# Strassen's seven block products in the first layer of the second expert pair, on one Trainium2 core

## The chip, the cores and the metric

The kernel runs on one core of one Trainium2 chip, as one program. The metric is the device time of one execution in microseconds (us); lower is better. Runs of the kernel before took 1161.63, 1161.28 and 1159.16 us, median 1161.28 us.

## What is computed

Retention over 768 steps for 4 x 8 heads of width 64, followed by two feed-forward layers ("expert pairs") on the 3072 resulting tokens of width 512:

```
state = gamma * state + k_t v_t^T ;  y_t = scale * q_t state        (per head)
x = y as 3072 tokens x 512
h = x @ w_in  (512 -> 2048);  g = h - tanh(h);  x = g @ w_out       (first pair)
h = x @ w2_in (512 -> 2048);  g = elu(h);       out = g @ w2_out    (second pair)
```

Inputs and outputs are float32. The four weight matrices arrive as doubles' bit patterns (int64), and the kernel makes float32 of them.

## The kernel before

Every float32 product is made of three float32r products: each operand is split into a high part (ACT copies it to float32r) and a low part (DVE subtracts the copy), and TensorE adds high x high, high x low and low x high in PSUM. Three matmuls of 128x128 by 128x512 therefore stand for one.

The 3072 tokens are six groups of 512 (`NB`), the 2048 hidden columns 16 pieces of 128 (`NF`). One *slot* is one group and one piece: `first_mm` (L268 to L279) makes h with 12 matmuls (four chunks of the inner size 512, three each), ACT and DVE make g of it (`act_tanhshrink` L289, `act_elu` L310), `split_hi` and `split_lo` (L281 to L287) split g, and `second_mm` (L328 to L343) adds g times the piece's row of the outer weights into four PSUM accumulators with 12 more matmuls. `second_mm` of a slot runs two slots behind `first_mm` (`SKEW`). There are 96 slots in each pair. In the first pair the slots of groups 0 and 1 are cut in two halves of eight pieces (`FA`), so that weights can be converted while they arrive.

The main loop (L577 to L619) writes the instructions of each engine in the order of the slots, and every engine runs its own list in that order, waiting on semaphores. Retention steps 4 to 23 are spread over the slots of the first pair by a table (`events`, L526 to L542): step s makes scores on TensorE (L164), masks on DVE (L172), outputs (L208, L215) and a state update (L237, L260, L263) for which the keys are scaled first (`att_scale_k`, L145). Steps 0 to 3 and the conversion of the first weights stand ahead of the loop, written out by hand (L399 to L502).

Weights are fetched (L81), converted on ACT and DVE (L86, L93, L94), split (L106, L107) and then stay in on-chip memory: one tag per piece for the inner and one for the outer weights, so that the second pair's weights replace the first pair's piece by piece during the last token group of the first pair. Between the pairs the tokens go through DRAM (`x1d`), and are loaded and split again, one group ahead (`load_x1` L380, `split_x1` L386). PSUM has eight banks: four accumulators, two for h, two for retention. All loads and stores are issued from SP's queue, except two that add into DRAM (POOL) and four tables (ACT).

The line at which the last output leaves is L359 behind the copies of L353.

Of the kernel before, what the change touches and what calls it, by code (L numbers as in the profile page):

```python
# [7 lines left out]
F32 = mybir.dt.float32  # L8
# [29 lines left out]
def retention_moe_kernel(ctx: ExitStack, tc: tile.TileContext, dims, ins, out):  # L41
# [10 lines left out]
    assert H * D == DM and 2 * D == P and B == SPB and NB == NCH and S % P == 0  # L52

    const = ctx.enter_context(tc.tile_pool(name="const", bufs=1))
    wp = ctx.enter_context(tc.tile_pool(name="wp", bufs=1))
    xp = ctx.enter_context(tc.tile_pool(name="xp", bufs=1))
    stg = ctx.enter_context(tc.tile_pool(name="stg", bufs=4))
    att = ctx.enter_context(tc.tile_pool(name="att", bufs=2))
    att1 = ctx.enter_context(tc.tile_pool(name="att1", bufs=1))
    tmp = ctx.enter_context(tc.tile_pool(name="tmp", bufs=1))  # L60
    ps_acc = ctx.enter_context(tc.tile_pool(name="ps_acc", bufs=1, space=PSUM))
    ps_h = ctx.enter_context(tc.tile_pool(name="ps_h", bufs=2, space=PSUM))
    ps_a = ctx.enter_context(tc.tile_pool(name="ps_a", bufs=1, space=PSUM))
# [8 lines left out]


    wts = {}
    raw = {}
    w32 = {}

    def fetch(m, f):

        raw[m, f] = wp.tile([P, TB], I64, tag=f"w{m % 2}_{f}", name=f"raw{m}_{f}")  # L80
        nc.sync.dma_start(out=raw[m, f], in_=ins[f"w{m}"][f])  # L81

    def convert_a(job):

        w = w32[job] = stg.tile([P, TB], F32, tag="w32", name=f"w32_{job[0]}_{job[1]}")
        nc.scalar.activation(out=w, in_=raw[job].bitcast(F32)[:, 1::2], func=AF.Prelu, scale=REBIAS, alpha=NEG)  # L86

    def convert_b(job):

        r, w = raw[job].bitcast(U32), w32[job]  # L90
        wu = w.bitcast(U32)
        return [
            lambda: nc.vector.tensor_single_scalar(wu, wu, 3, op=ALU.logical_shift_left),  # L93
            lambda: nc.vector.scalar_tensor_tensor(  # L94
                out=wu, in0=r[:, 0::2], scalar=29, in1=wu,
                op0=ALU.logical_shift_right, op1=ALU.bitwise_or,
            ),
        ]
# [12 lines left out]

    xhl = {}
    st = {}
    qkv_t = {}
    pt_t = {}

    def bank(s, part):

        tag = {"sc0": "a0", "sc1": "a1", "o": "a0"}[part]
        if s < B:  # L120
            tag = [("a0", "a1", "acc0"), ("acc1", "acc2", "acc3")][s % 2][("sc0", "sc1", "o").index(part)]
        return ps_acc if tag[:3] == "acc" else ps_a, tag

    def att_load(s, qk):
        nc.sync.dma_start(out=qk, in_=ins["qkv"][s][:, 0:2, :])
        qkv_t[s] = [qk, None, None]

    def att_load_v(s):
        v = att.tile([P, TB], F32, tag="v", bufs=B, name=f"v{s}")
        nc.sync.dma_start(out=v, in_=ins["qkv"][s][:, 2, :])  # L130
        qkv_t[s][1] = v

    def att_scale_q(s):
        q = qkv_t[s][0][:, 0, :].rearrange("p (a i) -> p a i", a=NP)
        nc.vector.tensor_tensor(out=q, in0=q, in1=qtab, op=ALU.mult)

    def att_load_kn(s, kn=None):
        if s // B == NCH - 1:
            return
        if kn is None:  # L140
            kn = att.tile([P, TB], F32, tag="kn", name=f"kn{s}")
        nc.sync.dma_start(out=kn, in_=ins["qkv"][s][:, 3, :])
        qkv_t[s][2] = kn

    def att_scale_k(s):  # L145
        if s // B == NCH - 1:
            return
        k = qkv_t[s][2].rearrange("p (h d) -> p h d", h=H)
        nc.vector.tensor_tensor(out=k, in0=k, in1=ktab.to_broadcast([P, H, D]), op=ALU.mult)

    def att_scores(s):
        t = qkv_t[s][0]
        if s < B:
            pt = tmp.tile([P, 2, NP, P], F32, tag="g", bufs=G_BUFS, name=f"pt{s}")
        else:
            pt = att1.tile([P, 2, NP, P], F32, tag="pt", name=f"pt{s}")
        sc = []
        for j in range(2):
            pool, tag = bank(s, f"sc{j}")
            sc.append(pool.tile([P, NP, P], F32, tag=tag, name=f"sc{s}_{j}"))  # L160
        for p in range(NP):
            for j in range(2):
                r = slice(j * D, (j + 1) * D)
                nc.tensor.matmul(  # L164
                    out=sc[j][:, p, :],
                    lhsT=t[r, 1, p * P:(p + 1) * P],
                    rhs=t[r, 0, p * P:(p + 1) * P],
                    start=True, stop=True,
                )
# [517 lines left out]
```

## Time and profile before

| | |
|---|---|
| median of three runs | 1161.28 us |
| the runs | 1161.63, 1161.28, 1159.16 us |
| span of the profiled execution | 1159.1 us (the page gives no other time of it; the nearest run is 1159.16) |
| TensorE (PE) busy | 1138.6 us, 98% |
| VectorE (DVE), ScalarE (ACT) busy | 684.6 us (59%), 625.2 us (54%) |
| moved by DMA | 80.44 MB, mean 69 GB/s |

The span runs from the first to the last instruction. A busy share is a mean over stages that differ; what a stage waits for is read in that stage, from the windows, the timeline and the waits. Matmuls overlap: the mean duration of one (about 390 ns) is longer than the distance between the starts of two, and only that distance adds up to time.

### The profile page before, as it was taken

The page shows a single profiled execution, that of the slowest core. Times are in us where ns is not written, and L with a number is a line of the kernel's source. Part 1 is how long each engine was busy: PE and PEld are TensorE (multiplying, and loading weights), DVE is VectorE, ACT ScalarE, POOL GpSimd, SP SyncE. Part 2 cuts the span into 40 slices and gives each one's busy share as a digit, 9 for nine tenths or more (in the row PEclk, how much of TensorE's full clock was granted, in tenths as well). Part 3 has the DMA queues.
Part 4 walks back from the last instruction along what each step waited for, and adds up shares of the span by engine and source line. Part 5 has one row for each costly group of instructions (what it writes and reads, how often), then busy time and mean ns, then how long its engine had stood idle before and what let it go on. Part 6 is the DMA issues. An engine that isn't in the chain of part 4 may idle for free.

```text
span 1159.1 us, 15702 instructions
## 1 busy us (share of the span) xinstructions
PE 1138.6 (98%) x6033; PEld 929.9 (80%) x6033; DVE 684.6 (59%) x1153; ACT 625.2 (54%) x1117; POOL 5.6 (0%) x10
## 2 busy tenths in 40 slices
PE   7799999999999999999999999999999999999998
PEld 5578887888888888888888888888888888888886
DVE  6898887657666665665798675343343343343332
ACT  2657785445545455455787765444444444444434
POOL 0000001000000000000000000000000000000000
PEclk9899999999999999999999999999999999999999
DMA  9930032431103102001675200200200200200000
GB/s 329 416 155 37 1 110 51 132 72 38 38 1 109 38 28 92 28 1 32 206 234 166 90 1 1 72 1 1 72 1 1 72 1 1 73 1 1 36 1 37
DMA packets 27562, 80.44 MB, mean 69 GB/s; under 512 B 3168, under 2 KB 3168, under 8 KB 27488
## 3 DMA queue, kind: packets, MB, share of 16 engines
q1 hardware_dynamic: 26048, 76.56, 19.0%
q0 software_dynamic: 864, 2.10, 1.2%
q8 instruction: 47, 0.77, 0.3%
q10 hardware_dynamic: 576, 0.79, 0.2%
q14 instruction: 27, 0.22, 0.1%
HBM read 64.76 MB, written 14.68 MB: 69 GB/s over the span
## 4 chain that ended last, share of the span: by engine, by line
PE 93%; DMA 3%; DVE 2%; ACT 0%; issue 0%; SPq 0%; DVEq 0%; ACTq 0%
PE acc L340 45%; PE h L274 43%; DMA raw<-w 2%; PE sc L164 2%; PE oe L215 1%; PE oe L208 1%; PE oo L215 1%; DMA stage<-qkv 1%; PE oo L237 1%; DMA dtab<-dtab 1%; DVE w L94 0%; DVE w L107 0%; SPq L81 0%; DVE v L307 0%; DVE x L227 0%
## 5 line engine op out<-in xcount | busy, mean ns | idle before, releaser
L340 PE MATMUL acc<-g,w 128*128 128x512 f32 x1152 | 282.0, 393 | 0.0
L274 PE MATMUL h<-x,w 128*128 128x512 f32 x1152 | 278.3, 391 | 0.0
L340 PE MATMUL acc<-w,g 128*128 128x512 f32 x1152 | 276.7, 389 | 0.6 <-DVE g L287 0.6
L274 PE MATMUL h<-y,w 128*128 128x512 f32 x1152 | 276.7, 389 | 0.0
L274 PEld LDWEIGHTS h<-x,w 128*128 128x128 f32 x1152 | 216.8, 188 | 45.5 <-issue 0.2
L340 PEld LDWEIGHTS acc<-w,g 128*128 128x128 f32 x1152 | 216.1, 188 | 45.9 <-DVE g L287 1.0
L274 PEld LDWEIGHTS h<-y,w 128*128 128x128 f32 x1152 | 216.2, 188 | 44.9
L340 PEld LDWEIGHTS acc<-g,w 128*128 128x128 f32 x1152 | 213.3, 188 | 47.3 <-ACT v L295 0.7
L320 DVE SCALAR_TENSOR_TENSOR v<-v,t 128x512 f32<-128x512 f32 x96 | 66.5, 693 | 298.7 <-ACT t L318 298.7
L315 ACT ACTIVATE u<-h 128x512 f32<-128x512 f32 x96 | 57.5, 599 | 259.5 <-PE h L274 258.1
L294 ACT ACTIVATE u<-h 128x512 f32<-128x512 f32 x96 | 57.5, 599 | 235.5 <-issue 224.4
L300 DVE SCALAR_TENSOR_TENSOR v<-v,u 128x512 f32<-128x512 f32 x96 | 66.5, 692 | 135.1 <-ACT v L295 135.1
L287 DVE TENSOR_TENSOR g<-v,g 128x512 fp32r<-128x512 f32 x192 | 131.5, 685 | 0.8 <-ACT g L283 0.8
L283 ACT ACTIVATE g<-v 128x512 fp32r<-128x512 f32 x192 | 118.2, 615 | 3.3 <-DVE v L323 2.0
L307 DVE COPY_PREDICATED v<-m,h 128x512 f32<-128x512 uint16 x96 | 70.4, 734 | 4.8 <-DVE h L306 0.5
L295 ACT ACTIVATE v<-u,qa_b 128x512 f32<-128x512 f32 x96 | 69.5, 724 | 3.1
L303 DVE SCALAR_TENSOR_TENSOR v<-v,h 128x512 f32<-128x512 f32 x96 | 65.6, 683 | 9.4 <-ACT t L297 9.4
L298 ACT ACTIVATE m<-u,xs_b 128x512 bf16<-128x512 f32 x96 | 68.3, 712 | 0.0
L306 DVE TENSOR_TENSOR h<-h,t 128x512 f32<-128x512 f32 x96 | 66.5, 693 | 0.0
L323 DVE TENSOR_TENSOR v<-h,v 128x512 f32<-128x512 f32 x96 | 65.7, 684 | 0.0
L316 ACT ACTIVATE v<-u 128x512 f32<-128x512 f32 x96 | 60.7, 632 | 3.1
L318 ACT ACTIVATE t<-u 128x512 f32<-128x512 f32 x96 | 59.3, 618 | 0.0
(54 smaller groups left out, 617.9 us busy)
## 6 DMA issues: line engine op xcount, KB each, us to landing
raw<-w SPq DMA_DIRECT2D x64, 512.0 KB, 5.6
qk<-qkv SPq DMA_DIRECT2D x20, 512.0 KB, 5.3
v<-qkv SPq DMA_DIRECT2D x24, 256.0 KB, 6.3
x<-x1d SPq DMA_DIRECT2D x12, 512.0 KB, 5.9
kn<-qkv SPq DMA_DIRECT2D x20, 256.0 KB, 6.0
out<-o SPq DMA_DIRECT2D x10, 512.0 KB, 2.9
x1d<-o SPq DMA_DIRECT2D x8, 512.0 KB, 3.0
stage<-qkv SPq DMA_DIRECT2D x4, 512.0 KB, 6.8
```

Of the source, the lines that this page charges most:

```text
L274: nc.tensor.matmul(out=h, lhsT=w[:, a, c * P:(c + 1) * P], rhs=x[:, b, c, :], start=(i == 0), stop=(i == 3 * KC - 1),)
L283: nc.scalar.activation(out=t[:, 0, :], in_=g, func=AF.Copy)
L287: nc.vector.tensor_tensor(out=t[:, 1, :], in0=g, in1=t[:, 0, :].bitcast(F32), op=ALU.subtract)
L295: nc.scalar.activation(out=v, in_=u, func=AF.Square, bias=qa_b)
L298: nc.scalar.activation(out=big, in_=u, func=AF.Relu, bias=xs_b)
L300: lambda: nc.vector.scalar_tensor_tensor(out=v, in0=v, scalar=QB, in1=u, op0=ALU.add, op1=ALU.mult),
L303: lambda: nc.vector.scalar_tensor_tensor(out=v, in0=v, scalar=C2, in1=h, op0=ALU.mult, op1=ALU.mult),
L306: lambda: nc.vector.tensor_tensor(out=h, in0=h, in1=th, op=ALU.subtract),
L307: lambda: nc.vector.copy_predicated(out=v, mask=big.bitcast(U16), data=h),
L320: lambda: nc.vector.scalar_tensor_tensor(out=v, in0=v, scalar=1.0, in1=th, op0=ALU.add, op1=ALU.mult),
L323: lambda: nc.vector.tensor_tensor(out=v, in0=h, in1=v, op=ALU.max),
L340: nc.tensor.matmul(out=acc[e], lhsT=lhsT, rhs=rhs, start=(f == lo and i == 0), stop=(f == hi - 1 and i == 2),)
```

## The change

The first layer of the second pair is computed for pairs of token groups and pairs of pieces at once. The tokens of groups 2p and 2p+1 are regrouped: the first halves of both groups make one block row of 512 tokens, the second halves the other; the inner size 512 is cut in two halves of 256, and pieces j and j+8 are the two block columns. The 2x2 block product is done with Strassen's seven products (in Winograd's form, with 15 additions) in place of eight. Each of the seven has two inner chunks of 128, so six matmuls. There are 3 pairs x 8 *quads* x 7 products.

- The sums of the weights (T1 to T4) and all splits are made once, in the third to sixth token group of the first pair (`weight_quad`), and written to DRAM (`w2d`); each quad loads its 14 blocks (1.8 MB) into one of two buffers in each of the three pairs.
- The sums of the tokens (S1 to S4) are made when a pair's tokens are loaded (`tokens`): seven operands, each split in a high and a low part.
- The sums of the products are made partly in PSUM (P1, P6, P5 and P3 add up in one bank) and partly by three copies to SBUF on ACT (`snap`) and three additions on DVE (`plus`) per quad.
- A quad gives four h blocks. The two of the first block row go at once through elu, split and the second layer (12 matmuls each, called tails, one quad later). The two of the second block row are stored after elu (`ys`) and go through split and second layer after the eighth quad, in 16 units of 12 matmuls.
- The outer weights of both pairs (`w1d`, `w3d`) are converted and split once, stored to DRAM, and loaded again for each use: 64 loads for groups 2 to 5 of the first pair, 96 for the second pair, five buffers each.
- The order of everything behind the hand-written start is no longer that of the code: the code records operations with their operands, durations and due times (`Plan.op`), TensorE's in a fixed order, and `Plan.run` lays out the other engines' operations by their latest useful start, as engines, buffers and operands come free in its own clock. What the hand-written start has fetched counts there as present at its time zero. TensorE's order in the first pair is the one of before.

The core of the new code (L643 and on; `op` records, `dma` records a transfer):

```diff
+        def weight_store(job, d):
+            t = W[job]
+            dma(lambda: nc.sync.dma_start(out=d.bitcast(F32), in_=t.ap.bitcast(F32)), 4096, r=[t], w=[dbuf(d)], due=FAR)
...
+            op("DVE", q, lambda: sub(T(0), hi_.ap[:, 0:HW], lo_.ap[:, 0:HW]), r=[lo_, hi_], w=[(t, 0)], name="T1")
+            op("DVE", q, lambda: sub(T(1), hi_.ap[:, HW:], T(0)), r=[hi_, (t, 0)], w=[(t, 1)], name="T2")
+            op("DVE", q, lambda: sub(T(2), hi_.ap[:, HW:], hi_.ap[:, 0:HW]), r=[hi_], w=[(t, 2)], name="T3")
+            op("DVE", q, lambda: sub(T(3), lo_.ap[:, HW:], T(1)), r=[lo_, (t, 1)], w=[(t, 3)], name="T4")
...
+            op("DVE", 1.14, lambda: sub(s3.ap, a11.ap, a21.ap), r=[a11, a21], w=[s3], name="S3")
+            op("DVE", 1.14, lambda: add(a21.ap, a21.ap, a22.ap), r=[a22], w=[a21], name="S1")
+            op("DVE", 1.14, lambda: sub(a21.ap, a21.ap, a11.ap), r=[a11], w=[a21], name="S2")
+            op("DVE", 1.14, lambda: sub(a21.ap, a12.ap, a21.ap), r=[a12], w=[a21], name="S4")
...
+        def product(i, q, xs, dst, first, last):
+            h, l = xs[i]
+            k = PLACE[i]
+            def fn():
+                for c in range(2):
+                    three(dst.ap, lambda a: q.ap[:, 7 * a + k, c * P:(c + 1) * P],
+                          lambda b: (h, l)[b].ap[:, c, :], first, last, 2, c)
...
+                xb, wb, zb = (Buf("P", [P, TB], F32, f"{c}{nm}") for c in "xwz")
+                product(1, q, xs, xb, True, True)
+                s1 = snap(xb, f"s1_{nm}")
+                product(2, q, xs, wb, True, True)
+                c11 = plus(wb, s1, f"c11_{nm}")
+                product(6, q, xs, xb, False, True)
+                u2 = snap(xb, f"u2_{nm}")
+                product(7, q, xs, zb, True, True)
+                z7 = snap(zb, f"z7_{nm}")
+                product(5, q, xs, xb, False, True)
+                c22 = plus(xb, z7, f"c22_{nm}")
+                product(4, q, xs, zb, False, True)
+                c21 = plus(zb, u2, f"c21_{nm}")
+                y11 = elu(c11, f"11{nm}")
+                g = split_g(y11, f"11{nm}")
+                if j < NQ - 1:
+                    filler()
+                product(3, q, xs, xb, False, True)
+                y12 = elu(xb, f"12{nm}")
+                g2 = split_g(y12, f"12{nm}")
+                elu(c21, f"21{nm}", ys, 0, 0)
+                elu(c22, f"22{nm}", ys, 1, 1)
+                filler()
```

**Place one: TensorE, one quad (the sixth of the middle pair).** Names: x1_5, w1_5 and z1_5 are the quad's three PSUM banks, xh and xl the high and low part of a token operand (xh6 is S2), q1_5 the weight blocks, acc3a the accumulators of the tails. Before, the same stretch of the second pair alternates 12 matmuls of h and 12 into the accumulators:

```order
L274 MATMUL h2_120_6697<-y1_5997,w2_8_5435 128x512 x12
L340 MATMUL acc112_0_6496<-w3_6_5977,g118_6679 128x512 x3
L340 MATMUL acc112_1_6497<-w3_6_5977,g118_6679 128x512 x3
L340 MATMUL acc112_2_6498<-w3_6_5977,g118_6679 128x512 x3
L340 MATMUL acc112_3_6499<-w3_6_5977,g118_6679 128x512 x3
```

Now, the third and fourth product of the quad and the beginning of the first tail:

```order
L392 MATMUL x1_5_8023<-xh6_1_7288,q1_5_7881 128x512
L392 MATMUL x1_5_8023<-xl6_1_7302,q1_5_7881 128x512
L392 MATMUL x1_5_8023<-xh6_1_7288,q1_5_7881 128x512 x2
L392 MATMUL x1_5_8023<-xl6_1_7302,q1_5_7881 128x512
L392 MATMUL x1_5_8023<-xh6_1_7288,q1_5_7881 128x512
L392 MATMUL z1_5_8063<-xh7_1_7205,q1_5_7881 128x512
L392 MATMUL z1_5_8063<-xl7_1_7211,q1_5_7881 128x512
...
L392 MATMUL acc3a1_0_7605<-w3_4_7922,g111_4_7975 128x512 x3
L392 MATMUL acc3a1_1_7610<-w3_4_7922,g111_4_7975 128x512 x3
```

A product is six matmuls in place of the twelve of an h, and a tail uses the g of the quad before.

**Place two: ACT, the same quad.** s1, u2 and z7 are the copies out of PSUM, u, y, t the three steps of an elu, g a split's high part; 111, 121, 211 and 221 are the four blocks of the middle pair. Before, each slot has four ACT instructions:

```order
L315 ACTIVATE u143_7570<-h2_143_7557 128x512
L316 ACTIVATE v143_7572<-u143_7570 128x512
L283 ACTIVATE g142_7575<-v142_7536 128x512
L318 ACTIVATE t143_7571<-u143_7570 128x512
L315 ACTIVATE u144_7606<-h2_144_7593 128x512
```

Now, from the first copy of the quad to the copy of z7:

```order
L288 ACTIVATE s1_1_5_8046<-x1_5_8023 128x512
L744 ACTIVATE ys1_4_8030<-u221_4_8020 128x512
L744 ACTIVATE t221_4_8057<-u221_4_8020 128x512
L744 ACTIVATE u111_5_8061<-s1_1_5_8046 128x512
L288 ACTIVATE u2_1_5_8070<-x1_5_8023 128x512
L744 ACTIVATE y111_5_8073<-u111_5_8061 128x512
L744 ACTIVATE t111_5_8083<-u111_5_8061 128x512
L288 ACTIVATE z7_1_5_8085<-z1_5_8063 128x512
```

The three copies stand between the steps of elus, and u2 stands behind the first step of c11 (which DVE makes in the tile of s1).

**Place three: DVE at the end of the hand-written start.** kn5 are the keys of retention step 5, v0 or y0 the first slot's value, w32 a weight before its split. Before:

```order
L94 SCALAR_TENSOR_TENSOR w32_1_0_349<-raw1_0_149,w32_1_0_349 128x512
L300 SCALAR_TENSOR_TENSOR v0_403<-v0_403,u0_401 128x512
L93 TENSOR_SCALAR w32_0_3_407<-w32_0_3_407 128x512
L303 SCALAR_TENSOR_TENSOR v0_403<-v0_403,h0_0_361 128x512
L93 TENSOR_SCALAR w32_1_1_409<-w32_1_1_409 128x512
```

Now:

```order
L316 SCALAR_TENSOR_TENSOR w32_1_0_368<-raw1_0_168,w32_1_0_368 128x512
L343 TENSOR_TENSOR kn5_374<-kn5_374,ktab_68 128x512
L291 TENSOR_TENSOR w0_2_389<-w32_0_2_322,w0_2_389 128x512
L291 TENSOR_TENSOR w1_0_394<-w32_1_0_368,w1_0_394 128x512
L312 TENSOR_SCALAR w32_0_3_397<-w32_0_3_397 128x512
```

The scaling of kn5, which stood 28 instructions further back (behind the second slot's value and its conversions), is now the first instruction that the plan puts on DVE.

## Rows read from the trace of the kernel before

**Rows 1.** The page: span, and busy time of each engine.
```profile
span 1159.1 us, 15702 instructions
PE 1138.6 (98%) x6033; PEld 929.9 (80%) x6033; DVE 684.6 (59%) x1153; ACT 625.2 (54%) x1117; POOL 5.6 (0%) x10
```
**Rows 2.** Windows by stage: length, busy time (count) per engine, clock, DMA share, GB/s.
```profile
0.00:52.00 52.00, 39.19 (x386) 28.29 (x387) 38.73 (x72) 23.24 (x41) 0.20 (x4) 0.93 0.96 367
46.00:85.00 39.00, 35.11 (x282) 27.49 (x272) 36.82 (x68) 25.33 (x48) 0.00 (x0) 1.00 0.60 242
...
237.00:338.00 101.00, 101.00 (x639) 82.18 (x638) 65.93 (x113) 50.49 (x92) 1.73 (x2) 1.00 0.16 43
...
546.00:636.00 90.00, 90.00 (x399) 74.53 (x398) 77.95 (x135) 69.51 (x122) 0.00 (x0) 1.00 0.64 199
...
630.00:1150.00 520.00, 519.65 (x2293) 429.96 (x2291) 220.81 (x359) 257.68 (x461) 0.00 (x0) 1.00 0.07 25
```
**Rows 3.** Timeline, a second-pair slot: start, us, engine, instruction, idle before.
```profile
904.23 2.88 PE L274 MATMUL h<-y,w 128*128 128x512 f32 x12
...
906.95 2.88 PE L340 MATMUL acc<-w,g 128*128 128x512 f32 x12
...
907.21 0.60 ACT L315 ACTIVATE u<-h 128x512 f32<-128x512 f32 x1 [3.13 <-PE h L274]
907.84 0.63 ACT L316 ACTIVATE v<-u 128x512 f32<-128x512 f32 x1
...
908.90 0.62 ACT L318 ACTIVATE t<-u 128x512 f32<-128x512 f32 x1
...
909.55 0.69 DVE L320 SCALAR_TENSOR_TENSOR v<-v,t 128x512 f32<-128x512 f32 x1 [3.54 <-ACT t L318]
...
910.16 0.69 DVE L287 TENSOR_TENSOR g<-v,g 128x512 fp32r<-128x512 f32 x1
910.76 0.68 DVE L323 TENSOR_TENSOR v<-h,v 128x512 f32<-128x512 f32 x1
```
**Rows 4.** Timeline of TensorE at the end.
```profile
1150.26 5.28 PE L340 MATMUL acc<-w,g 128*128 128x512 f32 x22 [0.61 <-DVE g L287]
```
**Rows 5.** Groups by shape on DVE: busy time, mean ns, idle before.
```profile
L107 DVE TENSOR_TENSOR w<-w,w 128x512 fp32r<-128x512 f32 x64 | 42.9, 682 | 0.0
L93 DVE TENSOR_SCALAR w<-w 128x512 uint32<-128x512 uint32 x64 | 26.6, 420 | 0.0
L263 DVE TENSOR_TENSOR st<-oo,st 128x256 f32<-128x256 f32 x16 | 6.8, 424 | 0.5
```
**Rows 6.** The page: issues of weight loads, median us to landing.
```profile
raw<-w SPq DMA_DIRECT2D x64, 512.0 KB, 5.6
```
**Rows 7.** Windows: 4 us in the loaded start.
```profile
30.00:34.00 4.00, 4.00 (x44) 3.44 (x42) 2.91 (x7) 4.00 (x8) 0.00 (x0) 1.00 1.03 421
```
**Rows 8.** Timeline of DVE: the last instruction before the plan's first.
```profile
29.56 0.69 DVE L94 SCALAR_TENSOR_TENSOR w<-raw,w 128x512 uint32<-128x512 uint32 x1
```
**Rows 9.** Timeline of SP: issue of kn5.
```profile
30.75 0.33 SPq L142 DMA_DIRECT2D kn<-qkv  x1
```
**Rows 10.** Key loads (L142): DMA time.
```profile
DMA to landing us min/median/max: 3.2/6.0/9.2
```
**Rows 11.** Timeline of TensorE, 39 to 86 us, where it waited.
```profile
39.49 2.17 PE L164 MATMUL sc<-qk 64*128 64x128 f32 x16 [5.12 <-DMA qk<-qkv]
41.59 4.16 PE L274 MATMUL h<-x,w 128*128 128x512 f32 x12
...
48.40 0.69 PE L237 MATMUL oo<-v,kn 128*64 128x64 f32 x16 [1.02 <-DVE kn L149]
49.01 3.01 PE L340 MATMUL acc<-g,w 128*128 128x512 f32 x12
...
56.05 1.13 PE L164 MATMUL sc<-qk 64*128 64x128 f32 x14 [0.73 <-DVE st L263]
...
65.79 0.69 PE L237 MATMUL oo<-v,kn 128*64 128x64 f32 x16 [1.29 <-DVE kn L149]
...
85.33 2.88 PE L274 MATMUL h<-x,w 128*128 128x512 f32 x12
```

More of the change, by code (lines that the diff above doesn't have):

```diff
@@ L37, with __init__ @@
 NEG = -(2.0 ** 32)
+PLACE = {1: 0, 2: 1, 3: 2, 5: 3, 6: 4, 7: 5, 4: 6}
+class Buf:
+    def __init__(self, cls, shape=None, dtype=None, name="", group=None, ap=None, slot=None):
+        self.cls, self.shape, self.dtype, self.name, self.group = cls, shape, dtype, name, group
+        self.ap, self.slot = ap, slot
+        self.left = 0
+        self.held = slot is not None
+        self.w, self.rd = {}, {}
+class Op:
+    __slots__ = ("eng", "fn", "dur", "lat", "bufs", "deps", "users", "rel", "late", "n", "name", "wait", "pe", "due")
@@ L145, in att_scale_k @@
[L145 to L169, printed above, removed]
-        pt_t[s] = pt
-        masks = [
-            lambda j=j: nc.vector.tensor_tensor(out=pt[:, j], in0=sc[j], in1=dtab[:, j], op=ALU.mult)
-            for j in range(2)
-        ]
-        if s < B:
-            yield
-            for op in masks:
-                op()
-        else:
-            yield masks + [lambda: att_scale_q(s)]
@@ L182, in half, with pairs @@
+    def pairs():
+        return [(p, j, slice(j * D, (j + 1) * D)) for p in range(NP) for j in range(2)]
     def half(p, j):
@@ L402, in retention_moe_kernel, with load_kn, three @@
+    def load_kn(t, s):
+        nc.sync.dma_start(out=t, in_=ins["qkv"][s][:, 3, :])
+    def three(out_, lhs, rhs, first, last, n=1, at=0):
+        for i, (a, b) in enumerate(((0, 0), (0, 1), (1, 0))):
+            nc.tensor.matmul(
+                out=out_, lhsT=lhs(a), rhs=rhs(b), skip_group_check=True,
+                start=(first and at == 0 and i == 0), stop=(last and at == n - 1 and i == 2),
+            )
     with tc.manual_schedule():
-        zt = tmp.tile([P, TB], BF16, tag="m", name="warm")
+        zt = place("C", "m0", [P, TB], BF16, "warm")
@@ L412, in retention_moe_kernel @@
         warm(11)
-        stage = xp.tile([P, B, 2, TB], F32, tag="x1", name="stage")
-        qk0 = [stage[:, s] for s in range(B)]
+        stage = place("X", "x1", [P, B, 2, TB], F32, "stage")
         jobs0 = [(0, 0), (0, 1)]
@@ new lines, in second, with fn @@
+        def second(m, w, g, acc, first, last):
+            for e in range(4):
+                sl = slice(e * P, (e + 1) * P)
+                def fn(e=e, sl=sl):
+                    if m == 1:
+                        three(acc[e].ap, lambda a: w.ap[:, a, sl], lambda b: g.ap[:, b, :], first, last)
+                    else:
+                        three(acc[e].ap, lambda a: g.ap[:, a, sl], lambda b: w.ap[:, b, :], first, last)
+                op("PE", 3 * MM, fn, r=[w, g], w=[acc[e]], lat=0.2, name=f"second{g.name}_{e}")
@@ new lines, in plus, with out_place, at, filler @@
+        def plus(src, t, name):
+            op("DVE", DVE5, lambda: add(t.ap, src.ap, t.ap), r=[src], w=[t], name=name)
+            return t
+        def out_place(p, i):
+            rows = out.rearrange("(e s) d -> s e d", e=B)
+            def at(e, n):
+                c, bb = divmod(e, 2)
+                s0 = (2 * p + c) * P
+                e0 = 2 * i + bb
+                return rows[s0:s0 + P, e0:e0 + n, :], None, Buf("D")
+            return at
+        tails = []
+        def filler(k=1):
+            for _ in range(k):
+                if tails:
+                    tails.pop(0)()
@@ L626 @@
+        for o, t in plan.run():
+            for b in o.bufs:
+                if b.ap is None and b.cls != "D":
+                    b.ap = place(b.cls, b.slot, b.shape, b.dtype, b.name)
+            o.fn()
+    return plan
 def kernel(q, k, v, moe_w_in, moe_w_out, moe2_w_in, moe2_w_out):
```

1099 lines of the change are left out of this document (682 added, 417 removed).

## The prediction

> **What bounds the kernel now.** First the page's engine line: TensorE is busy for 98% of the span, VectorE for 59%, ScalarE for 54% [rows 1]. A mean over stages can hide another bound, so second the windows by stage [rows 2]. TensorE is idle for 12.8 us of the first 52 and for 3.89 us (39 − 35.11) from 46 to 85, where DVE is busy for 36.82 of 39 us, 94%. From 237 to 338 and from 546 to 636 it is never idle, though DVE is at 87% (77.95/90) in the latter and DMA at 199 GB/s. From 630 to 1150 it idles 0.35 of 520 us. The granted clock is 1.00 in all of these but the first, so 2.4 GHz. Behind the start the time is therefore the number of matmuls by the distance of their starts. Third the timeline gives that distance: an h's twelve begin at 904.23, the next twelve at 906.95, so 2.72 us for 12, **0.2267 us each** [rows 3].
>
> The sum is made against the profiled execution's 1159.1 us; the median of the runs is 2.2 us above it, and I add that at the end. What the measurement can tell from no change is about 0.2%, 2.3 us.
>
> **Removed.** The second pair's first layer had 96 x 12 = 1152 matmuls; now 3 pairs x 8 quads x 7 products x 6 = 1008, of the same 128x512 shape. 144 x 0.2267 = **−32.6 us**. At the end TensorE waited 0.61 us for the last g [rows 4]. The last 16 units now take values stored long before: **−0.6**.
>
> **Hand-offs inside a quad.** A quad is 42 + 24 matmuls, 14.96 us, a product 1.36 us. A new wait can come where a product adds into a bank that ACT must first have copied. Walk, from the start of p1: ACT began on a finished bank 907.21 − 904.23 = 2.98 us after the first of twelve matmuls [rows 3], so 1.62 after the first of six. s1 is copied 1.62 to 2.22 (0.60 as the row of u), and p6, third in the bank's order, begins at 2.72: 0.50 to spare. The product behind s1 is readable at 2.98, DVE adds c11 by 3.67 (0.69), its relu ends at 4.27; u2 runs 4.34 to 4.94, p5 begins at 5.44: 0.50. Exp and tanh end at 5.52 and 6.12 if nothing is left from the quad before; z7 is readable at 5.70, so runs to 6.72 at worst, and p4 begins at 6.80: 0.08. The next s1 stands behind eight ACT instructions that begin at about 12.50 and ends at 17.44, with p6 at 17.68: 0.24. ACT has 17 instructions, about 9.4 us of the 14.96; DVE 13, about 7.8. So each hand-off fits, with less than one instruction to spare. Bounds: 0; or three hand-offs a quad late by 0.62 − 0.24 = 0.38 (one more ACT instruction ahead), 1.1 x 24 = 27 us. I take **+1**, near the lower end, since ACT and DVE have over 5 us free in each quad.
>
> There is a rule that speaks against such an order. First the row: behind a wait of 5.12 us, 16 short matmuls took 2.17 us where 14 of them later took 1.13 (1.29 for 16, so 0.88 lost), and the next twelve 4.16 us where twelve at full speed show 2.88 (1.28 lost), 2.16 us in all; behind a wait of 1.02 us twelve took 3.01 [rows 11], and the clock from 46 to 85, with waits up to 1.29, was 1.00 [rows 2]. So short waits cost only themselves. The Trainium skill, "TensorE: Matmul & The Clock Gate", section "A second HAM failure mode: psum-queue depth-cycling", says that a kernel that cycles through PSUM banks each iteration, with small pauses of TensorE between groups, had its clock oscillate and lost throughput. By it each quad might lose such 2.16 us, and the sum would be +52 instead of +1; this trace does not bear it out.
>
> **Weight preparation** moves from the last group of the first pair into its third to fifth (about 237 to 546 us), where its results go to DRAM. DVE per outer piece: 0.42 [rows 5] and two of 0.60 (the distance of DVE starts, 910.76 − 910.16 [rows 3]), 1.62 x 16 = 25.9. Per quad: two conversions of 1.02, four sums of 0.42 (256 wide, L263 [rows 5]) and low parts of 0.60, 0.42 and 1.20: 5.94 x 8 = 47.5. Together 73.4 us on 309, so DVE goes from 65% (65.93/101 [rows 2]) to about 89%. The nearest row is 546 to 636, 87% with no idle TensorE: 0. The other bound is 46 to 85, 94% and 3.89 us in 39, which over 309 us is 31. I take **+1**. In the last group this work is gone and nothing waited there.
>
> **DMA.** In the second pair a quad loads 1.835 + 2 x 0.524 MB in 14.96 us, 193 GB/s, like 546 to 636 (199 [rows 2]). The heaviest stretch lies between quads of two pairs: 14 units, 38.1 us, with tokens 2.10, outputs 1.05, twelve outer pieces 6.29 and two quads 3.67 MB, 13.1 MB or 344 GB/s. Four microseconds at the start moved 421 GB/s [rows 7]; the stretch with the lowest rate per busy share among the loaded ones, 546 to 636, gives 199/0.64 = 311, which needs 42.1 us. The outer weights are five buffers ahead, 4 x 2.72 = 10.9 us, and such a load lands in 5.6 us [rows 6]. I take **0**; the other bound is 2 x 4.0 = 8.
>
> **The start.** TensorE's order and the loads up to kn5 are as before, but kn5's scaling is now DVE's next instruction after 29.56 + 0.69 = 30.25 [rows 8], and SP issued kn5's load only at 30.75 [rows 9]. Key loads land in 3.2 to 9.2 us [rows 10]; in this full stretch I take 9.2, so 39.95. DVE stands for some 9.7 us; behind it are w0_2's low part (done about 41.4; the third slot's h began at 41.59 [rows 11]), the conversions and the first slot's value. Its list then puts the masks of step 5 at 51, so the accumulation that began at 49.01 [rows 11] begins at about 52.5, +3.5. But DVE's later instructions on keys and state now stand early: the waits 1.02, 0.73, 1.29 and, 17 us on, 0.73 again [rows 11], 3.8 us in all, go. Added up to the eighth inner piece, DVE has its low part ready at 85.5 where that h began at 85.33 [rows 11]: **+0.3**. Bounds: −3.9 (all waits from 46 to 85 gone) and +9.7 (the hole in full).
>
> **Sum.** 1159.1 − 32.6 − 0.6 + 1 + 1 + 0 + 0.3 = 1128.2 us for a span, + 2.2 = **1130 us** as median.
>
> **Rivals.**
> - *Hand-offs late.* As costed, up to +27 more: 1136 to 1157. For it: 0.08 and 0.24 us of slack. Against: ACT 63% and DVE 52% busy in a quad.
> - *DMA late between pairs*: 1130 + 8 = 1138. For it: 344 GB/s against a mean of 367 in the first 52 us, where TensorE waited [rows 2]. Against: 421 [rows 7].
> - *The hole in the start stays*: 1130 + 9.7 − 0.3, about 1140. For it: DVE at 94% from 46 to 85 cannot make up much. Against: the waits that its order now avoids.
> - *Slower: u2 caught behind c11.* u2 stands behind c11's relu on ACT, and c11's sum on DVE behind the previous quad's 211 block. The walk leaves 0.57 us; a lag beyond it holds p5, and all of TensorE's list behind it, 24 times. If an exp, a tanh, a multiplication and a maximum of that block are still due (0.63 + 0.62 + 0.69 + 0.68 = 2.6 [rows 3]), the price is (2.6 − 0.57) x 24 = 49: 1179. It becomes slower than before beyond a lag of 0.57 + 31.3/24 = 1.87. Against it: these steps belong to work that has 5 us free per quad.
> - *The clock falls in every quad* at one of the hand-offs, each with the 2.16 us lost behind the wait of 5.12 [rows 11]: 24 x 2.16 = 52, about 1181, slower as well. Against it: waits up to 1.29 us left the clock at 1.00 [rows 2], and no hand-off is off by more.
>
> That the change does not do what it says is excluded by TensorE's order, which has 1008 of the products' matmuls.
>
> **How the numbers follow.** Forecast (own range 1123 to 1135, from −4 at the start and −2 for hand-offs and weights at nothing, to +5 of their bounds) 0.57; late hand-offs 0.14; DMA 0.09; hole 0.09; u2 0.08; clock 0.03. The range 1122 to 1148 holds the forecast, DMA, the hole and half of the late hand-offs. Faster by over 0.2%: all but the last two and a little of the hand-offs, 0.88; within, 0.02; slower 0.10.
>
> **What would show it.** In the profile after: TensorE's starts still 0.2267 apart; in a quad no idle time before p6, p5 or p4, or one whose releaser is ACT's s1, u2 or z7 (hand-offs). A gap on DVE at 30 to 40 us that ends with kn5's load, accumulation late by about 3.5 us near 50, and no waits for keys behind it. DVE near 89% from 237 to 546 with TensorE idle under 1 us per 100. TensorE idle on DMA at the ends of pairs would show the DMA rival. No wait for g at the end. It is wrong if TensorE idles more than 8 us behind the start, or if the h matmuls' distance grows.

## The result and the profile after

The changed kernel took 1131.59 us (median of four runs, 1130.84 to 1132.20) against 1161.24 us (four runs) before: ratio **0.9748**, 95% interval 0.9734 to 0.9762. The forecast was 1130, with a range of 1122 to 1148. The profiled execution has a span of 1130.1 us, where the sum had come to 1128.2.

The page of the kernel after, its engine line:

```profile
span 1130.1 us, 15594 instructions
PE 1109.5 (98%) x5889; PEld 903.7 (80%) x5889; DVE 781.4 (69%) x1274; ACT 664.7 (59%) x1194; POOL 3.8 (0%) x8
```

TensorE has 5889 matmuls in place of 6033 [rows 1], 144 fewer, and is still the bound. These are the windows of the kernel after, with the columns of [rows 2]; the last is the stretch between the quads of the first two pairs:

```profile
0.00:52.00 52.00, 35.33 (x332) 25.72 (x336) 31.39 (x58) 19.63 (x35) 0.20 (x4) 0.87 0.82 301
46.00:85.00 39.00, 33.44 (x275) 27.18 (x275) 37.49 (x71) 24.46 (x47) 0.00 (x0) 0.91 0.43 150
237.00:546.00 309.00, 309.00 (x1885) 250.87 (x1884) 260.75 (x454) 192.20 (x350) 1.74 (x2) 1.00 0.68 244
546.00:636.00 90.00, 90.00 (x399) 74.53 (x398) 71.60 (x104) 59.08 (x99) 0.00 (x0) 1.00 0.49 187
...
753.92:792.46 38.54, 38.54 (x172) 31.91 (x170) 20.77 (x24) 14.69 (x22) 0.00 (x0) 1.00 0.85 334
```

Of these windows only the start has got worse: TensorE is idle for 16.7 us of the first 52 us instead of 12.8. The weight preparation brought DVE to 84% from 237 to 546 us, and TensorE is never idle there. Between two pairs DMA moved 334 GB/s at a share of 0.85, without a wait.

The start of the kernel after: first DVE behind the hand-written part, then TensorE from 39 us. These are the lines that answer to [rows 8, 11].

```profile
31.36 0.69 DVE L316 SCALAR_TENSOR_TENSOR w<-raw,w 128x512 uint32<-128x512 uint32 x1
39.99 0.69 DVE L343 TENSOR_TENSOR kn<-kn,ktab 128x512 f32<-128x512 f32 x1 [7.95 <-DMA kn<-qkv]
40.60 1.29 DVE L291 TENSOR_TENSOR w<-w,w 128x512 fp32r<-128x512 f32 x2
...
49.69 1.28 DVE L297 TENSOR_TENSOR pt<-sc,dtab 128x512 f32<-128x512 f32 x2
50.88 0.69 DVE L339 TENSOR_TENSOR qk<-qk,qtab 128x512 f32<-128x512 f32 x1
```

```profile
39.40 2.08 PE L332 MATMUL sc<-qk 64*128 64x128 f32 x16 [3.27 <-DMA qk<-qkv]
41.41 4.75 PE L392 MATMUL h<-x,w 128*128 128x512 f32 x12
51.72 0.48 PE L356 MATMUL oe<-qk,st 64*64 64x128 f32 x2 [5.56 <-DVE qk L339]
...
55.49 3.02 PE L392 MATMUL acc<-g,w 128*128 128x512 f32 x12
58.34 2.88 PE L392 MATMUL h<-x,w 128*128 128x512 f32 x12
...
87.39 2.88 PE L392 MATMUL h<-x,w 128*128 128x512 f32 x12
```

DVE stands for 7.95 us until kn5 is there; this is the hole of the prediction. The scaled queries of step 5 (`qk`) come 21 instructions behind kn5, and TensorE waits 5.56 us for them, where it had no such wait before. The first accumulation begins at 55.49, 6.48 us later than before [rows 11]. At 87.39 begins the h that began at 85.33 [rows 11]: the delay has shrunk to 2.06 us, because the waits of the kernel before for keys and states [rows 11] are gone. Its last waits of this kind, from 176 to 179 us, are gone too, so that 1.19 us are left from then on.

One quad of the kernel after: TensorE at p4, the product into z, here and in the next quad; ACT with the copies u2 (the first line) and z7 (the last); and the weight loads around p4's first (PEld):

```profile
694.86 0.43 PE L392 MATMUL z<-xh,q 128*128 128x512 f32 x1
695.12 0.39 PE L392 MATMUL z<-xl,q 128*128 128x512 f32 x1
...
709.92 0.44 PE L392 MATMUL z<-xh,q 128*128 128x512 f32 x1
```

```profile
692.63 0.58 ACT L288 ACTIVATE u<-x 128x512 f32<-128x512 f32 x1
693.11 0.62 ACT L744 ACTIVATE y<-u 128x512 f32<-128x512 f32 x1
693.63 0.62 ACT L744 ACTIVATE t<-u 128x512 f32<-128x512 f32 x1
694.15 0.59 ACT L288 ACTIVATE z<-z 128x512 f32<-128x512 f32 x1
```

```profile
694.40 0.19 PEld L392 LDWEIGHTS x<-xh,q 128*128 128x128 f32 x1
694.78 0.19 PEld L392 LDWEIGHTS z<-xh,q 128*128 128x128 f32 x1 [0.19 <-ACT z L288]
694.89 0.19 PEld L392 LDWEIGHTS z<-xl,q 128*128 128x128 f32 x1
```

From one p4 to the next it takes 15.06 us, not 66 x 0.2267 = 14.96. The copy z7 ends at 694.74; p4's matmul begins at 694.86. But it is not the matmul that waits, it is its *weight load*, which elsewhere begins some 0.23 us ahead of its matmul. So each hand-off has about 0.2 us less to spare than a walk by matmuls gives. u2 costs p5 a little in the same way: the distances of its starts are 0.228 to 0.236 us instead of 0.2267.

**The account** by the spans: −32.6 for 144 matmuls; +2.06 for the start at 87 us, of which 0.87 come back by 179; −0.9 for the last wait [rows 4] and the slower matmul behind it; +3.0 for hand-offs (behind 625 us the starts are 0.22805 us apart on average over 2193 distances; in eight_products below, which has no such hand-offs, 0.22667); +0.4 between the last matmul's start and the end (4.31 against 3.94 us). Together −28.9; the spans differ by 29.0.

### The profile page after: what moved, and what is told of

Read it like the earlier page. It is cut to its first block, busy times and chain, and to the rows that moved or that the text cites. A ratio compares the mean times of both kernels' runs of the same rounds, so it can differ in the third digit from the quotient of the medians.

```text
span 1130.1 us, 15594 instructions
## 1 busy us (share of the span) xinstructions
PE 1109.5 (98%) x5889; PEld 903.7 (80%) x5889; DVE 781.4 (69%) x1274; ACT 664.7 (59%) x1194; POOL 3.8 (0%) x8
## 4 chain that ended last, share of the span: by engine, by line
PE 96%; DMA 3%; DVE 1%; ACT 0%; issue 0%; SPq 0%
PE acc L392 24%; PE h L392 22%; PE x L392 12%; PE acc3a L392 12%; PE acc3b L392 12%; PE z L392 6%; PE w L392 3%; PE sc L332 2%; PE oe L362 1%; PE oe L356 1%; DMA kn<-qkv 1%; PE oo L362 1%; PE oo L370 1%; DMA stage<-qkv 1%; DMA dtab<-dtab 1%; DMA raw<-w 1%
## 5 line engine op out<-in xcount | busy, mean ns | idle before, releaser
L288 ACT ACTIVATE g<-y 128x512 fp32r<-128x512 f32 x144 | 90.8, 631 | 123.8 <-DVE y L731 92.5
L392 PE MATMUL acc3a<-w,g 128*128 128x512 f32 x576 | 137.1, 389 | 0.0
L392 PE MATMUL x<-xh,q 128*128 128x512 f32 x384 | 134.8, 391 | 0.0
L291 DVE TENSOR_TENSOR g<-y,g 128x512 fp32r<-128x512 f32 x144 | 99.5, 691 | 46.9 <-ACT g L288 43.5
L392 PE MATMUL acc3b<-w,gb 128*128 128x512 f32 x576 | 131.7, 389 | 0.0
L392 PEld LDWEIGHTS acc3a<-w,g 128*128 128x128 f32 x576 | 108.1, 188 | 22.7
L392 PEld LDWEIGHTS acc3b<-w,gb 128*128 128x128 f32 x576 | 108.1, 188 | 22.5
L392 PEld LDWEIGHTS x<-xh,q 128*128 128x128 f32 x384 | 72.0, 188 | 17.2 <-DVE z L294 1.0
L392 PE MATMUL x<-xl,q 128*128 128x512 f32 x192 | 74.9, 390 | 0.0
L731 DVE COPY_PREDICATED y<-m,h 128x512 f32<-128x512 uint16 x96 | 70.6, 735 | 4.1 <-ACT m L720 0.9
```

The costliest lines, as they stand in the source:

```text
L288: nc.scalar.activation(out=out_, in_=in_, func=AF.Copy)
L291: nc.vector.tensor_tensor(out=out_, in0=a, in1=b, op=ALU.subtract)
L392: nc.tensor.matmul(out=out_, lhsT=lhs(a), rhs=rhs(b), skip_group_check=True, start=(first and at == 0 and i == 0), stop=(last and at == n ...
L731: op("DVE", 0.65, lambda: nc.vector.copy_predicated(out=y.ap, mask=m.ap.bitcast(U16), data=h.ap), r=[m, h], w=[y], due=9.0)
```

## Experiments

The theory (A) is that the gain is the 144 matmuls, less the hole in the start (net 2 us by 87 us) and hand-offs without slack (3 us). The rivals are: (B) the plan, the blocks or the weights in DRAM bear a part of the gain; (C) the start is set by loads that DVE's wait hides behind; (D) the uneven distances in a quad belong to the products. Each of the first four kernels is one edit of the changed kernel; the kernel before took 1160.37 us beside them.

**kn5_later**

```diff
-            op("DVE", DVE5, lambda: scale_k_(k.ap), w=[k], name=f"scalek{s}")
+            op("DVE", DVE5, lambda: scale_k_(k.ap), w=[k], rel=4 if s == B + 1 else 0, name=f"scalek{s}")
```

> The scaling of kn5 may go to DVE only when the plan has begun four TensorE operations, so it stands 14 DVE instructions later and DVE has no instruction on kn5 ahead of w0_2's low part. Theory (the 2.06 us by which TensorE is late at 87 us come from DVE's 7.95 us wait for kn5's load): the wait is gone from 32 to 40 us, TensorE's 5.56 us wait for the scaled queries of step 5 shrinks to about 1 us, TensorE is at or ahead of the kernel before at 85 us, and the time falls by 2 to 5 us, to 1126.5 to 1129.5. Rival (the start is set by the load of qk5, which TensorE waits for at 39 us, and DVE's wait is hidden behind it): within 0.7 us of 1131.6, with the wait of TensorE taken over by another load.

Measured: 1124.58 us, ratio to before 0.9689 (0.9675 to 0.9704). DVE and TensorE in its profile:

```profile
31.76 1.47 DVE L291 TENSOR_TENSOR w<-w,w 128x512 fp32r<-128x512 f32 x2
33.15 0.97 DVE L312 TENSOR_SCALAR w<-w 128x512 uint32<-128x512 uint32 x2
...
40.48 0.69 DVE L343 TENSOR_TENSOR kn<-kn,ktab 128x512 f32<-128x512 f32 x1 [1.57 <-DMA kn<-qkv]
```

```profile
39.93 2.08 PE L332 MATMUL sc<-qk 64*128 64x128 f32 x16 [4.01 <-DMA qk<-qkv]
41.94 4.71 PE L392 MATMUL h<-x,w 128*128 128x512 f32 x12
...
48.67 1.66 PE L392 MATMUL acc<-g,w 128*128 128x512 f32 x6
...
80.60 3.14 PE L392 MATMUL h<-x,w 128*128 128x512 f32 x12
```

The gain of some 7 us is more than the 2 to 5 expected. TensorE's wait of 5.56 us for the scaled queries is gone altogether, where about 1 us was expected to stay. The first accumulation is back at 48.67, and the h of 85.33 begins at 80.60, 4.7 us ahead of the kernel before: without the hole the plan's order gains 4.7 us by then, and the hole had turned this into 2.06 us of loss. So the hole cost 6.8 us. C falls: TensorE still waits for the load of qk5 (4.01 us instead of 3.27), and the gain came without it.

**tail_split**: half of the first tail is moved from behind p4 to ahead of p5.

```diff
+        pe = plan.pe
+        for i in range(len(pe) - 7):
+            if [o.name for o in pe[i:i + 3]] == ["p7", "p5", "p4"] and pe[i + 7].name == "p3":
+                pe[i + 1:i + 7] = pe[i + 3:i + 5] + pe[i + 1:i + 3] + pe[i + 5:i + 7]
         for o, t in plan.run():
```

> Half of the first tail of a quad (six matmuls, 1.36 us) is moved from behind p4 to ahead of p5, so that u2 and z7 have 1.36 us more. Theory (a quad takes 15.07 us instead of 66 x 0.2267 = 14.96 because the copies u2 and z7 end just when the weight loads of p5 and p4 want to begin): the uneven distances from p7's end to the tail (0.228 to 0.274 us) become 0.2267, a quad takes 14.96 to 14.98, and the time falls by 2 to 2.6 us, to about 1129.3. Rival (the uneven distances belong to the products themselves, to their operands or the change of bank): they stay, and the time is within 0.7 us of 1131.6.

Measured: 1129.85 us, 0.9731 (0.9717 to 0.9746), by the ratios 2.0 us under the changed kernel. The intervals overlap, so the trace has to decide; TensorE's p4 in its profile:

```profile
693.93 0.39 PE L392 MATMUL z<-xh,q 128*128 128x512 f32 x1
...
708.89 0.39 PE L392 MATMUL z<-xh,q 128*128 128x512 f32 x1
```

A quad takes 14.96 us, and the mean distance behind the first pair is 0.22710 in place of 0.22805, 2.1 us over 2193. (The span of this profile is 4.1 us shorter. The other 2.05 us came in the start, which the edit leaves alone: the first accumulation began at 53.44 instead of 55.49.) What is left over 0.25 us are distances in the last quad of each pair, whose order the edit doesn't touch. D falls: the same products, with time for the copies, run evenly.

**eight_products**

```diff
-                product(1, q, xs, xb, True, True)
-                s1 = snap(xb, f"s1_{nm}")
...
+                product(1, q, xs, c11, True, False)
+                product(2, q, xs, c11, False, True)
+                product(6, q, xs, c12, True, False)
+                product(5, q, xs, c12, False, True)
...
+                product(7, q, xs, c21, True, False)
+                product(4, q, xs, c21, False, True)
...
+                product(3, q, xs, c22, True, False)
+                product(1, q, xs, c22, False, True)
```

> Each quad takes eight products in place of seven, two for each block in a bank of its own, added up in PSUM alone; the three copies and three additions of a quad are gone; everything else (weights through DRAM, the plan, the stored second block row) stays. An eighth product repeats an operand, so the time is that of a blocked layer without Strassen, and the values are not those of the layer. Theory (the whole gain is the 144 matmuls less, and the rest of the change is worth within 3 us of nothing): 1131.6 + 32.6 - 2.6 for the hand-offs, 1161.6, between 1159 and 1165. Rival (a part of the gain is the new order, the blocks or the weights in DRAM): under 1155. Second rival (the blocked form has waits of its own for banks): over 1168.

Measured: 1161.65 us, 1.0009 (0.9999 to 1.0018). The kernel leaves out the copies and additions that put the seven products together, so its values are not those of the layer. With all the rest of the change in place the time is that of the kernel before, within 0.2%. B falls. Without copies every distance behind 625 us is 0.22 or 0.23 us, 0.22667 on average: the yardstick for the hand-offs.

**copies_twice**

```diff
-            op("ACT", ACT5, lambda: copy(t.ap, src.ap), r=[src], w=[t], name=name)
+            op("ACT", 2 * ACT5, lambda: (copy(t.ap, src.ap), copy(t.ap, src.ap)), r=[src], w=[t], name=name)
```

> Each of the three copies of a quad from PSUM is made twice by ACT, so that s1, u2 and z7 end 0.5 to 0.6 us later each; the plan, which is told of it, moves z7 ahead of one tanh. Theory (the hand-offs have 0.0 to 0.3 us of slack and what goes beyond it stops TensorE for just that long): TensorE waits 1.0 to 1.5 us per quad ahead of p6, p5 and p4, 24 to 36 us in all, 1156 to 1168, with the granted clock at 1.00. Rival one (ACT has five free us in each quad, and the order leaves room): under 1137. Rival two (short waits lower the clock): over 1180, with a granted clock below 0.95 from 640 us on.

Measured: 1152.58 us, 0.9931 (0.9915 to 0.9948), 21 us more than the changed kernel, less than the 24 expected at least and far from both rivals. ACT (s1, made twice) and TensorE at p6, the second product into x, of one quad, and the windows of two stretches of quads, columns as above:

```profile
693.04 1.21 ACT L288 ACTIVATE s<-x 128x512 f32<-128x512 f32 x2
```

```profile
693.74 0.39 PE L392 MATMUL w<-xh,q 128*128 128x512 f32 x1
694.31 0.50 PE L392 MATMUL x<-xh,q 128*128 128x512 f32 x1 [0.18 <-ACT s L288]
```

```profile
640.00:740.00 100.00, 98.77 (x416) 76.50 (x415) 52.95 (x81) 71.73 (x131) 0.00 (x0) 1.00 0.57 210
...
800.00:905.00 105.00, 103.45 (x434) 79.68 (x434) 54.74 (x84) 74.22 (x134) 0.00 (x0) 1.00 0.52 194
```

s1 ends at 694.25, the first matmul of p6 begins at 694.31, 0.57 us behind the one ahead of it: 0.35 us are lost. The next distance is 0.34, which loses another 0.11. The three hand-offs of this quad lose 0.45 + 0.21 + 0.26 us in this way. So a late copy costs its lateness and about 0.1 us more. A quad takes some 16.0 us instead of 15.07, and 0.93 x 24 = 22. Up to three waits in every quad left the granted clock at 1.00: the clock rival of the prediction falls. The Trainium skill ("TensorE: Matmul & The Clock Gate", section "A second HAM failure mode: psum-queue depth-cycling") tells of a bf16 kernel whose clock oscillated because TensorE paused briefly between its groups of matmuls, as it cycled through PSUM banks. This trace does not show that with waits of 0.1 to 0.35 us.

The next four have the changed kernel once more among them; the kernel before took 1160.76 us beside them.

**after_again**, no edit.

> The changed kernel once more, without an edit, on the chip and beside the runs of the three that follow: 1130.8 to 1132.2 by its own four runs. It fixes what a difference of 1 to 3 us in this set is measured against, and shows how far the start of one and the same kernel moves from run to run: the first outputs into the accumulators began at 55.49 us in one profile.

Measured: 1132.07 us, 0.9751 (0.9738 to 0.9764). The first accumulation began at 55.47, within 0.02 us of the other profile, so the hole is not a chance of one run. But in tail_split, with the same start, it began at 53.44, so a difference of 2 us in the start between two single profiles says nothing about an edit.

**sooner_split**: tail_split, and the loads of step 5 moved ahead of the eight weights.

```diff
+        qk[B + 1] = place("A", "qa", [P, 2, TB], F32, f"qk{B + 1}")
+        load_qk(qk[B + 1], B + 1)
+        kn[B + 1] = place("B", "kb", [P, TB], F32, f"kn{B + 1}")
+        load_kn(kn[B + 1], B + 1)
         for i in range(4, 12):
             fetch(i)
...
-        qk[B + 1] = place("A", "qa", [P, 2, TB], F32, f"qk{B + 1}")
-        load_qk(qk[B + 1], B + 1)
...
```

> The loads of qk5 and kn5 are issued ahead of the eight weight loads in the hand-written start, not behind them; kn5's scaling stays where the change put it, ahead of w0_2's low part. Half of the first tail stands ahead of p5 as in tail_split. Theory (the wait of 7.95 us on DVE is the load's landing, and any way to have kn5 earlier removes it; TensorE's own wait of 3.3 us for qk5 goes with it): no wait of DVE for kn5 beyond 1 us, the first accumulation at 44 to 47 us in place of 55.5, the whole 8 to 11 us under the changed kernel less 2.1 for the split, so 1119 to 1123. Rival (the weights, which are now 2 us later, become what TensorE waits for in the first slots): 1126 to 1131, with TensorE waiting for a weight of the fourth or a later slot.

Measured: 1122.02 us, 0.9667 (0.9654 to 0.9680). The time is as expected, the way there only in part. TensorE doesn't wait for qk5 at all, but DVE still waits 1.7 us for kn5, not under 1 us, and the first accumulation began at 48.97, not at 44 to 47:

```profile
PE oe L356 <- DVE qk L339: 6.6, 1, 6.6
```

TensorE now comes early to the queries of step 5 and waits 6.6 us for DVE to scale them: DVE's list, with its conversions, is the next bound of the start.

**all_mends**, sooner_split and kn5_later.

> The edits of kn5_later and of sooner_split together: kn5 loaded earlier and its scaling later, and the split tail. Theory (both edits of the start remove the same wait of DVE, so their gains do not add): within 1 us of sooner_split. Rival (the place of the instruction costs something of its own, in work that stands behind it): 2 us or more under sooner_split.

Measured: 1122.61 us, 0.9671 (0.9658 to 0.9684): no difference from sooner_split, as the theory has it. Its one profile (1120.0 us) is 2.0 us shorter: DVE's wait of 1.7 us for kn5 is gone in it, and the first accumulation begins at 46.97 instead of 48.97. The medians don't show these 2 us, and tail_split's start moved as much without an edit. So the bulk of the cost of the instruction's place is gone once its data comes early; whether up to 2 us of it stay is open.

**spare_loads**: with each load of an outer weight in the second pair goes a copy of it to one spare place in DRAM.

```diff
+            if m == 3:
+                dma(lambda: nc.sync.dma_start(out=spare.bitcast(F32), in_=d.bitcast(F32)), 4096, r=[dbuf(d)], rel=max(0, now_pe() - 12), due=0.0, name=f"spare{m}_{f}")
...
```

> With every load of an outer weight in the second pair goes a copy of the same 0.5 MB to a spare place in DRAM, issued when the list of TensorE comes near its use; nothing waits for the copies. Between the quads of two pairs the 13.1 MB in 38.1 us become 19 to 20 MB, over 500 GB/s if they were to stay in the stretch. Theory (the transfers of the change are hidden with a margin of a quarter of the DMA engines' time: the stretch after one pair shows a share of 0.75 at 300 GB/s): the share reaches 1.0 there, TensorE waits 3 to 10 us for an outer weight or a quad's weights at each of the two changes of pair, 1137 to 1150. Rival (the five buffers ahead and the lighter quads on both sides take it up): within 2 us of 1131.6.

Measured: 1190.80 us, 1.0259 (1.0243 to 1.0275), 59 us more: neither theory. What SP's queue and TensorE waited for (in all, times, longest), and the window of the first change of pair:

```profile
SPq L609 <- DMA spare<-w3d: 308.1, 78, 7.9
...
PE acc3b L393 <- DMA w<-w3d: 44.1, 24, 6.4
```

```profile
764.30:822.20 57.90, 38.41 (x146) 28.73 (x144) 19.44 (x23) 13.17 (x20) 0.00 (x0) 0.91 0.81 293
```

TensorE waited 44.1 us for outer weights, while DMA was busy for 81% and moved 293 GB/s, so the bytes were hardly the bound. All copies write the same place, so each waits for the one before, 78 times and 308 us in all; the theory now is that SP issues in order, and that the load behind a waiting copy waits with it. This experiment tested a wait, not bytes. Hence the next:

**spare_apart**: sixteen spare places in turn, so that the same bytes move without that wait. It and the two that follow ran beside 1160.72 us of the kernel before.

```diff
-    spare = dram.tile([P, 2, TB], F32R, name="spare")
+    n_spare = [0]
+    spare = [dram.tile([P, 2, TB], F32R, name=f"spare{i}") for i in range(16)]
...
```

> spare_loads with sixteen spare places in turn in place of one, so that a copy does not wait for the one before it, and SP, which issues in order, does not hold the loads behind it. The bytes are the same. Theory (the 59 us of spare_loads were SP waiting for one copy after the other, 308 us in all at a DMA share of only 0.79, and not the bytes): 1131 to 1145, with the share between 0.9 and 1.0 in the 38 us between the quads of two pairs and TensorE waiting there for at most 6 us each time. Rival (the bytes themselves were too many: copies from DRAM to DRAM take more than their share of the DMA engines): over 1170, with TensorE waiting for outer weights as before.

Measured: 1135.91 us, 0.9798 (0.9782 to 0.9815), 4.3 us more than the changed kernel in place of 59. The windows behind the first and the second pair:

```profile
753.00:793.00 40.00, 38.40 (x171) 31.49 (x169) 21.39 (x25) 15.88 (x23) 0.00 (x0) 1.00 0.98 389
918.00:958.00 40.00, 38.99 (x173) 31.99 (x172) 22.56 (x27) 16.48 (x24) 0.00 (x0) 1.00 0.96 379
```

Now DMA is full, at 389 GB/s, and TensorE waits 2.6 us for outer weights in both together; SP's queue waits 30.9 us for copies in all, not 308.1. The theory of SP's order holds. The changed kernel's 334 GB/s are some 86% of what this stretch carried here.

**prep_more**: DVE makes the last low part of each quad's weights five times.

```diff
+            for _ in range(4):
+                op("DVE", 1.14, lambda: sub(tl.ap, t.ap, th.ap.bitcast(F32)), r=[t, th], w=[tl])
```

> In each of the eight quads of the weight preparation DVE makes the last low part five times in place of once, four more instructions of some 1.28 us each (1.2 us apart), 38 to 41 us between 237 and 600 us. DVE was busy for 260.75 of the 309 us from 237 to 546, 84%. Theory (DVE has to be above about 95% for longer than a few slots before TensorE waits, since due work goes ahead of preparation): DVE at 92 to 97% there, 0 to 5 us more, 1132 to 1137. Rival (the bound used in the prediction, TensorE idle for 10% of a stretch in which DVE is at 94%): 15 to 31 us more, 1147 to 1163.

Measured: 1139.28 us, 0.9820 (0.9806 to 0.9835), 7.7 us more: between the two theories, in the range of neither. The windows, the last of them behind the second stop, and TensorE at its two stops:

```profile
237.00:330.00 93.00, 93.00 (x592) 75.56 (x592) 80.10 (x138) 55.27 (x101) 1.75 (x2) 1.00 0.60 200
330.00:420.00 90.00, 87.93 (x539) 71.02 (x536) 83.77 (x140) 54.39 (x99) 0.00 (x0) 0.98 0.67 242
420.00:546.00 126.00, 123.70 (x729) 99.31 (x728) 118.52 (x198) 77.72 (x142) 0.00 (x0) 1.00 0.73 260
...
427.00:546.00 119.00, 119.00 (x711) 95.96 (x710) 111.52 (x186) 73.75 (x135) 0.00 (x0) 1.00 0.72 258
```

```profile
343.44 0.50 PE L392 MATMUL acc<-g,w 128*128 128x512 f32 x1 [1.69 <-ACT g L288]
344.31 4.37 PE L392 MATMUL acc<-g,w 128*128 128x512 f32 x11 [0.38 <-DVE g L291]
...
423.89 0.50 PE L392 MATMUL acc<-g,w 128*128 128x512 f32 x1 [1.69 <-ACT g L288]
425.00 2.79 PE L392 MATMUL acc<-g,w 128*128 128x512 f32 x11 [0.60 <-DVE g L291]
```

With DVE at 86% TensorE doesn't wait. At 93% and 94% it waits 4.4 us for g, and behind the first stop it runs slower for a while, 4.37 us for eleven matmuls. Against the changed kernel it falls back by 7.2 us from 330 to 546, 3.3% of that stretch and not the 10% of [rows 2]. All of this comes at the two stops; behind the second, DVE is at 94% for 119 us (111.52 busy) and TensorE never waits. What sets the two places apart in the trace: ahead of each, DVE did nothing for a slot's value for 7.5 us (331.49 to 339.02 and 412.17 to 419.70), but weight preparation and retention; the next longest such time is 4.45 us, and no stop follows it. In the changed kernel the longest from 237 to 546 is 2.6 us. So by this trace it is preparation in one piece that costs, more than DVE's share; no run varies the one without the other.

**last_too**: all_mends, and half a tail ahead of p5 in the last quad of a pair as well.

```diff
+            if [o.name for o in pe[i:i + 4]] == ["p7", "p5", "p4", "p3"]:
+                pe[i + 1:i + 6] = pe[i + 4:i + 6] + pe[i + 1:i + 4]
```

> All edits that gained so far: qk5 and kn5 loaded ahead of the eight weights, kn5's scaling later, half a tail ahead of p5, now in the last quad of each pair too, where the distances at p7 to the tail were still up to 0.34 us. Theory (a late copy costs TensorE its wait and about 0.1 us more on the next matmul): the last distances over 0.25 us behind the first pair go, 0.2 to 0.3 us for each of three quads, so 0.6 to 1.2 us under all_mends, 1121 to 1122. Rival (the products p3 and p5 or the additions, which now stand closer together in the last quad, wait for DVE): 1123 or more.

Measured: 1123.01 us, 0.9682 (0.9668 to 0.9696), no gain over all_mends; the mean distance behind the first pair is 0.2271 us in both. TensorE from p4's last matmul to p3's first:

```profile
734.54 0.39 PE L392 MATMUL z<-xh,q 128*128 128x512 f32 x1
734.96 0.50 PE L392 MATMUL x<-xh,q 128*128 128x512 f32 x1
```

The uneven distances at p4 went, but p3, now directly behind p4, begins 0.42 us behind the matmul ahead of it: it adds into the bank that DVE has to have read for c22. The hand-off moved to another engine, as the rival said.

The fastest kernels of the study are sooner_split and all_mends, 3.3% under the kernel before and 0.8% under the changed one.

## Why the prediction was right

- **Removed matmuls** (−32.6): right; eight_products gives them back to within 0.2%.
- **The start** (+0.3): the mechanism was right, found from the order and the issue of kn5's load, and the size was off: 2.06 us at 87 us, 1.19 later. kn5 was there when worked out (39.99 us against 39.95), but DVE came to it later, so the hole was 7.95 us, not 9.7. The failed step is that the accumulation "begins at about 52.5, +3.5": it put only the masks of step 5 behind the hole, but the scaled queries stand behind them in DVE's list, and the first half of the step's output already needs these. TensorE stood until 51.72, worked at a granted clock of 0.52 to 55.49, so near the lower of its two levels (1.2 GHz; as behind the wait of 5.12 in [rows 11]), and the delay was 6.48. The waits given back were 4.4 by 87 us and 0.87 later, against the 3.8 taken, which were the idle times of [rows 11]. Behind 49.01 the idle time of [rows 11] is 2.75 us, and 4.4 came back: such a wait costs more than its idle time. The scores that waited for 0.73 us at 56.05 took 2.27 us from their first matmul to the next accumulation, and the same scores 1.09 us in the kernel after.
- **Hand-offs** (+1): 3.0. The walk gave p4 0.08 us to spare and did not take off the 0.2 us by which its weight load goes ahead. With that, z7 is late, as the trace shows.
- **Weight preparation** (+1): 0; DVE was at 84%, not 89%. The bound of 31 us, from 46 to 85, was far too high: prep_more lost 7.2 us in 216 at 93 to 94%, and nothing in the last 119 of them.
- **DMA** (0): right, 334 GB/s against the 344 worked out; spare_apart shows 389, above the 311 used as a bound, so the 8 us of the DMA rival (1138) rested on too low a rate.
- **u2 behind c11**: in the trace c11's relu held u2 back by 0.26 us, less than the 0.57 of the walk, so the rival that ends slower did not occur; copies_twice shows that such delays would be paid nearly in full.

The errors are +0.9 for the start by the end, +2 for hand-offs, −1 for preparation, −0.3 and +0.4 at the tail: the sum of 1128.2 lies 1.9 us under the span. That it is this close is in part luck: in the start 6.48 us of delay in place of 3.5 met 5.3 us of waits given back in place of 3.8, and the preparation, which cost nothing, made up for a part of the hand-offs. The size of the gain itself, the removed matmuls, is not luck.

## What to carry to other kernels

Where TensorE is the bound, a cut in matmuls is worth its number times the distance of their starts, provided that the copies which it brings end before the *weight load* of the product that needs the bank, and not just before its matmul. Other matmuls between a product and the one that adds to its bank give that room (tail_split), unless they bring the next user of a bank closer (last_too). When a planner takes over behind code written by hand, look at the first instructions that it puts on each in-order engine: what it counts as present may still be on its way, and everything behind waits with it. A transfer that waits on an issuing queue holds the ones behind it, so TensorE can wait for loads while DMA is at 81% (spare_loads). Background work is best spread out: in the trace of prep_more a busy share of 94% cost nothing over 119 us where no long piece of it stood ahead of due work.

## What had not been expected

- The wait for a bank falls on the weight load. In copies_twice the matmul behind a late one is 0.34 us away instead of 0.227, and most distances stay at 0.228 to 0.237 for the next ten matmuls or so; the reason is open.
- With waits of 0.1 to 0.35 us, up to three in a quad, the granted clock stayed at 1.00; behind waits of 3.3 to 4.0 us in the start twelve matmuls took 4.71 to 4.75 us instead of 2.88, behind the 1.02 us of [rows 11] twelve took 3.01. The two stops of prep_more are nearly equal and yet differ: behind 1.69 and 0.38 us eleven matmuls took 4.37 us at a granted clock of 0.66 (343.44 to 348.50), behind 1.69 and 0.60 us eleven took 2.79 at 1.00 (423.89 to 429.00). So the length of a stop alone does not say whether the clock falls.
- The planned order gains 4.7 us in the start, and one instruction placed too early hid that.
